# The first forty microseconds of an mLSTM kernel: gates loaded in two parts, differences moved into ScalarE's exponentials, one transposition cut in three

## The chip, the cores and the metric

One core of one Trainium2 chip runs the whole program. The metric is the device time of one execution in microseconds. TensorE (PE) multiplies matrices; PEld is its loading of weights; VectorE (DVE), ScalarE (ACT) and GpSimd (POOL) do the elementwise work; SyncE (SP) issues the DMAs.

## What is computed

Three stages follow one another; the change touches the start of the first. Per head (32 of them, 768 steps, dimension 40):

```python
for t in range(S):
    m_new = np.maximum(f_gate[:, :, t] + m, i_gate[:, :, t])
    f_stab = np.exp(f_gate[:, :, t] + m - m_new)
    i_stab = np.exp(i_gate[:, :, t] - m_new)
    m = m_new
    C = f_stab * C + i_stab * outer(v_t, k_t)
    n = f_stab * n + i_stab * k_t
    y[:, :, t] = sigmoid(o_gate) * (C @ q_t) / max(abs(n @ q_t), 1)
```

Then comes a soft mixture of experts over the 3072 tokens (softmax over tokens and over slots, 8 experts), then a two-layer network with a squared ReLU.

## The kernel before

The mLSTM is done in chunks of 128 steps: six chunks (NC = 6) for each of eleven groups of three heads. A unit is one group and one chunk. For a unit, TensorE spreads a row of gate sums over the partitions (`e_mb`, tile ps_mb), ScalarE makes weights of them with exponentials (`e_exp`, tile w), GpSimd clears the upper triangle (`e_sel`), TensorE multiplies keys with queries (`e_st`, tile ps_st), VectorE multiplies the two (`e_pm`, tile p), TensorE applies the result to the values (`e_av`, `e_inter`, tile ps_o) and updates the state (`e_u`, tile ps_st).

The gate rows (32 heads, three copies on 96 partitions) are prepared ahead for two chunks at a time by `prep(c0, c1)`: chunks 0 and 1 as "1", 2 and 3 as "2", 4 and 5 as "3". The order of all this is written out by hand in the string `START`, whose tokens are run one by one in program order; each engine then executes its own instructions strictly in that order. The part before the first `|` runs ahead of the loop over units; the parts behind it run one in each of the first turns of the loop. A token is:

- `~n`: n warming matmuls of TensorE, whose results nobody reads; they write the bank `ltb` (ps_lt).
- `1f`: scan of the forget gates (VectorE). `1i`: input gate less that sum. `1m`: copy of a carry and scan of the maximum. `1p`: the maximum carried in (mprev). `1h`: the negated maximum in bf16 (ScalarE). `1r`, `1u`, `1l`, `1v`: what bf16 left over, split into two more bf16 rows (VectorE, ScalarE, VectorE, ScalarE).
- `1a`, `1b`: two differences (G means GpSimd instead of VectorE), and `1A`, `1B`: their exponentials (ScalarE). `1q`: transposition of the three gate rows by TensorE into `ltb` and a copy out of it to `qt3`.
- `D0`: the four steps of the decay of a chunk pair, one at each call (VectorE and ScalarE; VectorE; TensorE; VectorE).
- `T`, `M`, `E`, `K`, `P` with a number: `e_st`, `e_mb`, `e_exp`, `e_sel`, `e_pm` of that unit. `W`: `e_wv`, the values times a gate column of `qt3` (GpSimd). `X`: a copy.

The loop begins with `e_u` of unit 0, then `e_mb` of unit 3 and `e_st` of unit 2, and so on. There are two ps_st banks; `e_u` of unit 0 takes the bank that `e_pm` of unit 0 (P0) has just read. The keys are loaded in three blocks of a group (one DMA for each head j) and in two halves of the sequence; the blocks off the diagonal of `kbd` (in par0 and par1, par_70 and par_71 in the instruction rows) are cleared to zero first. DMAs use eight semaphores in turn (DMAHW0 to DMAHW7): SyncE issues the ninth when the first has landed, and so on.

Of the kernel before, what the change touches and what calls it, by code (L numbers as in the profile page):

```python
# [13 lines left out]
AF = mybir.ActivationFunctionType  # L14
# [3 lines left out]
NEG = -1e30  # L18
# [14 lines left out]
W8 = 1  # L33
WO = (3, 6, 9)
LAST = {3: "PADNgGG", 2: "gGGA", 1: ""}
START = "~36 1f 1i 1m 1h 1p 1b 1aG 1B 1r 1u 1A 1v D0 2f 1l T0 T1 1q M0 2i E0 W0 K0 D0 M1 E1 ~6 2m D0 2p 2b 2aG K1 W2 P0 2h D0 2B 2r 2u P1 M2 2v E2 2A 2l K2 ~7 | 3f 3i D1 ~6 | D1 2q 3m 3h 3p | D1 3b 3aG 3B 3r | 3u D1 3A 3l 3v | D2 3q | D2 | D2 | D2 X |"
REBIAS = 2.0**-112


# [5 lines left out]
def kernel(  # L45
# [231 lines left out]
    nc.sync.dma_start(out=fg.rearrange("p c s -> p (c s)"), in_=f_gate)  # L277
    nc.sync.dma_start(out=ig.rearrange("p c s -> p (c s)"), in_=i_gate)
    halves = slice(0, S // 2), slice(S // 2, S)
    nc.vector.memset(kbd[0][:, :, halves[0]], 0.0)  # L280
    for g, cs in ((1, halves[0]), (0, halves[1]), (1, halves[1])):
        z = kbd[g][:, :, cs]
        nc.scalar.activation(z, ident[0 : 3 * D, 0:1].unsqueeze(2).to_broadcast(list(z.shape)), AF.Copy, scale=0.0)
    for g in range(2):
        load_kb(g, halves[0])
        load_q(g, halves[0])
        load_kv(g)
    for g in range(2):
        load_kb(g, halves[1])
        load_q(g, halves[1])  # L290
    nc.sync.dma_start(out=phs, in_=phi)
    load_x(0, range(NC))
# [101 lines left out]

    def prep_dec(c0, c1):
# [1270 lines left out]
```

## Time and profile before

| | us |
|---|---|
| median of three runs (378.13 to 380.14) | 379.23 |
| the profiled execution | 378.38 |
| its span on the core | 376.6 |

The profiled execution took 378.38 us, of which its span is 376.6 us and 1.8 us lie around it. It is 0.85 us below the median. Times in the rows are counted from the start of the span.

### The profile page before, as it was taken

Reading aid. Unit: us, or ns where it says so; the run is one execution under the profiler, and the core shown is the slowest. Engines: PE = TensorE matmul, PEld = TensorE weight load, DVE = VectorE, ACT = ScalarE, POOL = GpSimd, SP = SyncE. Lnnn points to the kernel's source line nnn. Section 1 sums busy time; section 2 is a strip of 40 time slices with the busy share of each in tenths; the row PEclk is TensorE's granted clock in tenths of the full one; section 3 lists DMA queues with packets and bytes.
Section 4 is the critical chain, followed back from the end, with each engine's and each line's share of the span. In section 5 each row is a group of like instructions: output and inputs, shape, how many; then the busy total and the mean of one; then the engine's idle time right before and its main releaser. Section 6 shows DMA issues by size and latency. Waiting matters only on the chain.

```text
span 376.6 us, 10714 instructions
## 1 busy us (share of the span) xinstructions
PE 364.9 (97%) x4203; PEld 324.9 (86%) x4203; DVE 264.7 (70%) x597; ACT 259.0 (69%) x594; POOL 99.8 (26%) x205
## 2 busy tenths in 40 slices
PE   7999998999999999999999999999999999999996
PEld 6789887888879885345899999999999999999995
DVE  7979888979998487786799655555555555555551
ACT  7798775669666865775798766576576666667661
POOL 5666976766677474000000000000000000000000
PEclk9999999999999999999999999999999999999999
DMA  6797997899969999994000100020020002002002
GB/s 175 248 333 231 286 328 212 275 317 372 319 190 400 339 365 297 342 376 177 3 0 2 62 9 1 2 70 0 2 70 2 1 2 70 3 0 71 0 3 70
DMA packets 19547, 56.72 MB, mean 151 GB/s; under 512 B 2481, under 2 KB 7561, under 8 KB 19113
## 3 DMA queue, kind: packets, MB, share of 16 engines
q1 hardware_dynamic: 19497, 56.04, 43.6%
q8 instruction: 33, 0.54, 0.6%
q14 instruction: 17, 0.14, 0.1%
HBM read 52.10 MB, written 3.93 MB: 149 GB/s over the span
## 4 chain that ended last, share of the span: by engine, by line
PE 81%; DVE 9%; POOL 3%; issue 3%; ACT 1%; DMA 1%; SPq 0%; DVEq 0%; POOLq 0%
PE ps_mb L1561 19%; PE ps_st L1561 17%; PE ps_lt L1561 9%; PE ps_st L474 8%; PE ps_o L1488 4%; PE ps_o L559 3%; PE ps_o L574 3%; PE ps_st L1376 2%; PE ps_st L502 2%; DVE p L486 2%; PE ps_m L1488 2%; PE ps_mb L443 2%; DVE x L656 1%; PE ps_lt L725 1%; PE ps_st L1224 1%
## 5 line engine op out<-in xcount | busy, mean ns | idle before, releaser
L1512 DVE CAST hi<-ring 128x512 fp32r<-128x512 f32 x93 | 39.7, 427 | 62.0 <-ACT ring L1511 51.8
L1513 DVE TENSOR_TENSOR los<-ring,hi 128x512 fp32r<-128x512 f32 x96 | 66.4, 692 | 9.8
L457 ACT ACTIVATE w<-ps_mb,qt 128x128 f32<-128x128 f32 x192 | 56.3, 366 | 15.1 <-PE ps_mb L443 7.5
L1493 ACT ACTIVATE ring<-ps_o 128x512 f32<-128x512 f32 x64 | 38.3, 598 | 35.0 <-PE ps_o L1488 35.0
L1511 ACT ACTIVATE ring<-ring 128x512 f32<-128x512 f32 x93 | 58.8, 632 | 3.0
L474 PE MATMUL ps_st<-par 120*128 120x128 f32 (+1 forms) x384 | 56.9, 284 | 0.7 <-DMA par<-in_q_t_dram 0.6
L1561 PE MATMUL ps_mb<-wohlh,hi 128*128 128x320 f32 x160 | 49.5, 310 | 0.0
L1561 PE MATMUL ps_mb<-wohll,hi 128*128 128x320 f32 x160 | 49.3, 309 | 0.0
L1561 PE MATMUL ps_mb<-wohlh,los 128*128 128x320 f32 x160 | 49.2, 309 | 0.0
L474 PEld LDWEIGHTS ps_st<-par 120*128 120x128 f32 (+1 forms) x384 | 47.9, 192 | 1.1 <-DVE ring L370 0.9
L1561 PE MATMUL ps_st<-wohll,hi 128*128 128x320 f32 x144 | 44.7, 310 | 0.0
L1561 PE MATMUL ps_st<-wohlh,hi 128*128 128x320 f32 x144 | 44.6, 309 | 0.0
L1561 PE MATMUL ps_st<-wohlh,los 128*128 128x320 f32 x144 | 44.5, 309 | 0.0
L464 POOL TENSOR_SCALAR_AFFINE_SELECT w<-w 128x384 f32<-128x384 f32 (+1 forms) x66 | 36.4, 551 | 17.1 <-ACT w L457 11.2
L486 DVE TENSOR_TENSOR p<-ps_st,w 128x384 f32<-128x384 f32 (+1 forms) x66 | 35.5, 537 | 4.2 <-POOL w L464 3.3
L1493 ACT ACTIVATE ring<-ps_m 128x512 f32<-128x512 f32 x32 | 19.2, 600 | 19.0 <-PE ps_m L1488 19.0
L1561 PEld LDWEIGHTS ps_mb<-wohll,hi 128*128 128x128 f32 x160 | 29.9, 187 | 1.5
L1561 PEld LDWEIGHTS ps_mb<-wohlh,los 128*128 128x128 f32 x160 | 30.0, 188 | 0.0
L1561 PEld LDWEIGHTS ps_mb<-wohlh,hi 128*128 128x128 f32 x160 | 30.0, 188 | 0.0
L1561 PEld LDWEIGHTS ps_st<-wohll,hi 128*128 128x128 f32 x144 | 27.0, 187 | 2.1 <-issue 0.6
L1561 PEld LDWEIGHTS ps_st<-wohlh,los 128*128 128x128 f32 x144 | 27.1, 188 | 0.0
L1561 PEld LDWEIGHTS ps_st<-wohlh,hi 128*128 128x128 f32 x144 | 27.1, 188 | 0.0
(318 smaller groups left out, 760.7 us busy)
## 6 DMA issues: line engine op xcount, KB each, us to landing
ring<-in_w_dram SPq DMA_DIRECT2D x22, 640.0 KB
stage<-in_w_in_dram SPq DMA_DIRECT2D x10, 512.0 KB
par<-in_w_dram SPq DMA_DIRECT2D x6, 640.0 KB
out_dram<-ring SPq DMA_DIRECT2D x24, 160.0 KB
par<-in_v_s_dram SPq DMA_DIRECT2D x9, 369.0 KB
par<-in_k_s_dram SPq DMA_DIRECT2D x9, 360.0 KB
x<-in_o_gate_dram SPq DMA_DIRECT2D x9, 320.0 KB
par<-in_k_t_dram SPq DMA_DIRECT2D x23, 120.0 KB
```

Of the source, the lines that this page charges most:

```text
L457: nc.scalar.activation(w[:, j, :], mb[:, 128 * j : 128 * j + 128], AF.Exp, bias=qt3[:, c, h0 + j : h0 + j + 1])
L464: nc.gpsimd.affine_select(out=w, in_=w, pattern=[[0, nh], [1, 128]], compare_op=ALU.is_ge, fill=0.0, base=0, channel_multiplier=-1)
L474: nc.tensor.matmul(st[:, 128 * j : 128 * j + 128], lhsT=kbd[g % 2][0:nd, j, ts_], rhs=qin[g][0:nd, ts_], start=True, stop=True,)
L486: nc.vector.tensor_tensor(out=p, in0=sts.pop((g, c))[:, 0 : nh * 128].rearrange("p (n t) -> p n t", n=nh), in1=ws.pop((g, c)), op=ALU.mult,)
L559: nc.tensor.matmul(pos[g, c // 2][:, o0 : o0 + nv], lhsT=qin[g][0:nd, 128 * c : 128 * c + 128], rhs=cbds[g, c - 1][0:nd], start=True, stop ...
L574: nc.tensor.matmul(po[t0 : t0 + 32, o0 : o0 + DV], lhsT=p[:, j, t0 : t0 + 32], rhs=vin[g][:, c, j, :], start=True, stop=True,)
L1488: nc.tensor.matmul(t, lhsT=gst[n][:, 128 * k : 128 * k + 128], rhs=cst[tg], start=True, stop=True)
L1493: nc.scalar.activation(r, t, AF.Relu)
L1511: nc.scalar.activation(r, r, AF.Square)
L1512: nc.vector.tensor_copy(hi, r)
L1513: eng.tensor_tensor(out=lo, in0=r, in1=hi.bitcast(F32), op=ALU.subtract)
L1561: nc.tensor.matmul(acc[u][:, 0:DM], lhsT=l_[:, 128 * u : 128 * u + 128], rhs=wohl[r_, f // 8][:, f % 8, :], start=(f == 0 and a == 0), sto ...
```

## The change

The gates are loaded for chunks 0 and 1 first and for the other four later, v and k of the first two groups likewise; the rest of the loads stand in `load_second`, token `L`. The clearings by ScalarE become six of one head each, and the last clearing goes to GpSimd. The two differences `a` and `b` are gone: the exponentials take them as bias, with one instruction for each chunk, and a small negation `1n` takes their place. The transposition of the first chunk pair becomes three (`1s` for the first 32 rows through bank m, `1t` for the second, `1w` for the third through `ltb`), of which the second and third are copied out by VectorE. Two reductions and a copy of VectorE (`heads`, token `H`) move from the front into the sequence. `START` is written anew.

```diff
-START = "~36 1f 1i 1m 1h 1p 1b 1aG 1B 1r 1u 1A 1v D0 2f 1l T0 T1 1q M0 2i E0 W0 K0 D0 M1 E1 ~6 2m D0 2p 2b 2aG K1 W2 P0 2h D0 2B 2r 2u P1 M2 2v E2 2l 2A K2 ~7 | 3f 3i D1 ~6 | D1 2q 3m 3h 3p | D1 3b 3aG 3B 3r | 3u D1 3A 3l 3v | D2 3q | D2 | D2 | D2 X |"
+START = "~13 1f 1i 1s ~9 1m 1h 1p 1n 1r 1u 1v H D0 1l T0 T1 ~1 1B 2f M0 1t E0 2i W0 K0 D0 M1 E1 ~5 2m 2h 2p 2n P0 H D0 2r D0 1A 2u K1 W2 P1 M2 2v E2 2l 2A K2 1w L ~7 | 3f 3i D1 2B ~6 | D1 2q 3m 3h 3p 3n | D1 3A 3r | 3u D1 3B 3l 3v | D2 3q | D2 | D2 | D2 X |"
...
+    def load_gates(c0, c1):
+        for t, src in ((fg, f_gate), (ig, i_gate)):
+            nc.sync.dma_start(
+                out=t[:, c0:c1].rearrange("p c s -> p (c s)"), in_=src[:, L * c0 : L * c1]
+            )
+
+    def zero(g, j, cs):
+        z = kbd[g][:, j, cs]
+        nc.scalar.activation(z, ident[0 : 3 * D, 0:1].to_broadcast(list(z.shape)), AF.Copy, scale=0.0)
+
+    load_gates(0, 2)
...
+    for g in (1, 0):
+        for j in range(3):
+            zero(g, j, halves[1 - g])
+    load_kb(0, halves[0])
+    load_q(0, halves[0])
+    load_kv(0, 0, 2)
+    load_gates(2, NC)
+    load_kb(1, halves[0])
+    load_q(1, halves[0])
+    load_kv(1, 0, 2)
...
-        nc.vector.tensor_copy(selF[rs, :], ident[rs, rs])
-    nc.vector.tensor_copy(sel96, selF[0:96])
+        if r < 3:
+            nc.vector.tensor_copy(sel96[rs, :], ident[rs, rs])
+        nc.gpsimd.tensor_copy(selF[rs, :], ident[rs, rs])
+    nc.gpsimd.memset(kbd[1][:, :, halves[1]], 0.0)
...
-        def qt():
+        def qt(r=0, n=96):
             t = ltb
             for c in range(c0, c1):
-                nc.tensor.transpose(t[:, 96 * (c - c0) : 96 * (c - c0) + 96], q3[:, c, :], ident[0:96, 0:96])
-            nc.scalar.copy(qt3[:, cs, :], t[:, 0 : 96 * w].rearrange("p (c s) -> p c s", s=96))
+                nc.tensor.transpose(t[:, n * (c - c0) : n * (c - c0) + n], q3[0:n, c, :], ident[0:n, 0:n])
+            tv = t[:, 0 : n * w].rearrange("p (c s) -> p c s", s=n)
+            (nc.vector.tensor_copy if r else nc.scalar.copy)(qt3[:, cs, r:n], tv[:, :, r:])
...
         def exp(r):
-            return lambda: nc.scalar.activation(q3[r : r + 32, cs], q3[r : r + 32, cs], AF.Exp)
+            def go():
+                for c in range(c0, c1):
+                    src, b, k = (q3, mlast, 1.0) if r == 32 else (mm, mprev, -1.0)
+                    nc.scalar.activation(
+                        q3[r : r + 32, c], src[r : r + 32, c], AF.Exp, bias=b[r : r + 32, c], scale=k
+                    )
+
+            return go
```

Three places in the engines' instruction streams. The first is TensorE's, from the third decay step of the first chunk pair (L410, L455 after) to `e_u` of unit 0 (L502, L547 after); lines left out are `e_mb` and further warming matmuls. Before:

```order
L410 MATMUL ps_m<-ring 120x22 [waits DVE_49]
...
L443 MATMUL ps_mb<-M_112,sel_105 128x128
L200 LDWEIGHTS ident
L200 MATMUL ps_lt<-ident 128x256
...
L502 MATMUL ps_st<-wv,par_70 120x123 [waits DMAHW7_49,DVE_49]
```

In the changed kernel the same stretch has the transpositions of `1w` (L374) in it:

```order
L455 MATMUL ps_m<-ring 120x22 [waits DVE_49,PE_49]
...
L374 MATMUL ps_lt<-ident,ring 128x96 [waits Activation_49] x2
L200 LDWEIGHTS ident
L200 MATMUL ps_lt<-ident 128x256 [waits DVE_49]
...
L547 MATMUL ps_st<-wv,par_70 120x123 [waits DMAHW7_49,PE_49,Pool_49]
```

What moved: a transposition now stands ahead of the seven warming matmuls of `~7`, it uses their bank, and the first of them now waits for VectorE.

The second place is VectorE's, from P0 (L531, `p<-ps_st,w`) on. In the changed kernel:

```order
L531 TENSOR_TENSOR p<-ps_st,w 128x384 [waits Pool_49]
L350 COPY ring<-ring 32x120
L419 SCALAR_TENSOR_TENSOR ring<-ring,M_112 96x256 [waits Activation_49]
L463 COPY dec_114<-ps_m 120x11x2 [waits PE_49]
L531 TENSOR_TENSOR p<-ps_st,w 128x384 [waits Pool_49]
L401 TENSOR_TENSOR M_112<-ring,M_112 32x256 [waits Activation_49]
L376 COPY qt_113<-ps_lt 128x2x32 [waits PE_49]
L563 TENSOR_TENSOR ring<-ps_st,hm 120x123 [waits PE_49]
```

Before, the same place reads (L486 is P0 and P1, L376 is `2r`, L370 is `2l`):

```order
L486 TENSOR_TENSOR p<-ps_st,w 128x384 [waits PE_49,Pool_49]
L418 COPY dec_114<-ps_m 120x11x2 [waits PE_49]
L376 SCALAR_TENSOR_TENSOR ring<-ring,M_112 96x256 [waits Activation_49]
L486 TENSOR_TENSOR p<-ps_st,w 128x384 [waits Pool_49]
L370 TENSOR_TENSOR M_112<-ring,M_112 32x256 [waits Activation_49]
L518 TENSOR_TENSOR ring<-ps_st,hm 120x123 [waits PE_49]
```

What moved: the copy of `heads` (L350) came in behind P0, and the copy out of `1w` (L376) behind `2l`.

The third place is GpSimd's, around W0 (L475, `wv<-par_70,qt`) in the changed kernel; L343 are the copies taken over from VectorE, L344 is the clearing of the second half of par_71, L509 is K0 and K1.

```order
L338 COPY selJ<-ident 32x4x8 [waits Pool_49]
L343 COPY selF<-ident 32x32 x4
L344 MEMSET par_71 120x3x384 [waits DMAHW3_49,DMAHW4_49,Activation_49,Pool_49]
L475 TENSOR_TENSOR wv<-par_70,qt_113 128x246 [waits DMAHW6_49,DVE_49]
L509 AFFINE_SELECT w<-w 128x384 [waits Activation_49] x2
```

Before, between the copy to selJ and W0 stood the difference `1a`; now a clearing stands there that waits for two DMAs, the key blocks of heads j = 1 and 2 of group 1 (the eleventh and twelfth loads, DMAHW3 and DMAHW4).

## Rows read from the trace of the kernel before

**Rows 1.** The page, the chain that ended last: shares by engine.
```profile
PE 81%; DVE 9%; POOL 3%; issue 3%; ACT 1%; DMA 1%; SPq 0%; DVEq 0%; POOLq 0%
```

**Rows 2.** The chain from 0 to 60 us: start us, us, what.
```profile
1.25 3.77 DMA ring<-in_i_gate_dram
...
5.11 0.42 DVE ring L370
...
11.63 0.57 DVE p L486
...
12.24 0.47 PE ps_st L502 x2
...
13.02 0.91 PE ps_st L474 x6
13.93 0.66 PE ps_lt L200 x6
...
22.03 0.40 DVE p L486
...
22.68 0.48 PE ps_o L559 x2
```

**Rows 3.** VectorE's groups, 0 to 14 us: busy us, mean ns of one, idle before.
```profile
L376 DVE SCALAR_TENSOR_TENSOR ring<-ring,M 96x256 f32<-96x256 f32 x2 | 1.5, 738 | 0.0
L360 DVE TENSOR_TENSOR_SCAN ring<-ring 96x256 f32<-96x256 f32 x2 | 1.4, 717 | 0.1
...
L370 DVE TENSOR_TENSOR ring<-ring 32x256 f32<-32x256 f32 x2 | 1.2, 602 | 0.1
L486 DVE TENSOR_TENSOR p<-ps_st,w 128x384 f32<-128x384 f32 x2 | 1.1, 550 | 0.0
...
L370 DVE TENSOR_TENSOR ring<-ring 96x256 f32<-96x256 f32 x2 | 0.8, 421 | 0.3 <-DMA ring<-in_i_gate_dram 0.2
L370 DVE TENSOR_TENSOR M<-ring,M 32x256 bf16<-32x256 f32 x2 | 0.8, 416 | 0.1
...
L321 DVE COPY ring<-ring 32x120 f32<-32x120 f32 x1 | 0.3, 266 | 0.0
...
L418 DVE COPY dec<-ps_m 120x22 f32<-120x22 f32 x1 | 0.2, 171 | 0.0
```

**Rows 4.** GpSimd's groups, 0 to 14 us.
```profile
L430 POOL TENSOR_TENSOR wv<-par,qt 128x246 f32<-128x246 f32 x2 | 1.4, 717 | 3.7 <-ACT qt L351 2.4 <-DMA par<-in_v_s_dram 1.3
L464 POOL TENSOR_SCALAR_AFFINE_SELECT w<-w 128x384 f32<-128x384 f32 x2 | 1.1, 531 | 0.1
L303 POOL MEMSET ring<- 96x768 f32 x1 | 0.7, 738 | 0.0
```

**Rows 5.** Timeline, 0 to 22 us: SyncE's issues and TensorE's first e_st.
```profile
2.15 2.92 SPq L210 DMA_DIRECT2D par<-in_k_t_dram  x3
...
5.12 0.36 SPq L215 DMA_DIRECT2D par<-in_q_t_dram  x1
...
5.52 0.43 SPq L225 DMA_DIRECT2D par<-in_v_s_dram  x1
...
7.70 1.57 PE L474 MATMUL ps_st<-par 120*128 120x128 f32 x12 [0.61 <-DMA par<-in_q_t_dram]
```

**Rows 6.** Timeline, 0 to 22 us: a copy out of ps_lt, what follows, W0 and `2p`.
```profile
9.48 0.32 ACT L351 COPY qt<-ps_lt 128x192 f32<-128x192 f32 x1 [0.17 <-PE ps_lt L350]
...
9.85 0.82 PE L200 MATMUL ps_lt<-ident 128*128 128x256 bf16 x6
...
9.93 0.83 POOL L430 TENSOR_TENSOR wv<-par,qt 128x246 f32<-128x246 f32 x1 [2.37 <-ACT qt L351]
...
10.41 0.38 DVE L365 TENSOR_TENSOR ring<-ring 96x2 f32<-96x2 f32 x1
```

**Rows 7.** The warming matmuls' durations (min/median/max ns), in 2 to 3 us.
```profile
L200 PE MATMUL ps_lt<-ident x7: 417/418/418, 1.6 to 2.9; 128*128 128x256 bf16 x7
```

**Rows 8.** The same, in 5 to 6 us.
```profile
L200 PE MATMUL ps_lt<-ident x12: 272/273/273, 4.7 to 5.9; 128*128 128x256 bf16 x12
```

More of the change, by code (lines that the diff above doesn't have):

```diff
@@ L35 @@
 LAST = {3: "PADNgGG", 2: "gGGA", 1: ""}
-START = "~36 1f 1i 1m 1h 1p 1b 1aG 1B 1r 1u 1A 1v D0 2f 1l T0 T1 1q M0 2i E0 W0 K0 D0 M1 E1 ~6 2m D0 2p 2b 2aG K1 W2 P0 2h D0 2B 2r 2u P1 M2 2v E2 2A 2l K2 ~7 | 3f 3i D1 ~6 | D1 2q 3m 3h 3p | D1 3b 3aG 3B 3r | 3u D1 3A 3l 3v | D2 3q | D2 | D2 | D2 X |"
+START = "~13 1f 1i 1s ~9 1m 1h 1p 1n 1r 1u 1v H D0 1l T0 T1 ~1 1B 2f M0 1t E0 2i W0 K0 D0 M1 E1 ~5 2m 2h 2p 2n P0 H D0 2r D0 1A 2u K1 W2 P1 M2 2v E2 2l 2A K2 1w L ~7 | 3f 3i D1 2B ~6 | D1 2q 3m 3h 3p 3n | D1 3A 3r | 3u D1 3B 3l 3v | D2 3q | D2 | D2 | D2 X |"
 REBIAS = 2.0**-112
@@ L276, with load_second @@
     nc.scalar.activation(dm, dm, AF.Exp)
-    nc.sync.dma_start(out=fg.rearrange("p c s -> p (c s)"), in_=f_gate)
-    nc.sync.dma_start(out=ig.rearrange("p c s -> p (c s)"), in_=i_gate)
+    def load_gates(c0, c1):
[7 more added lines that the diff above has]
+    load_gates(0, 2)
     halves = slice(0, S // 2), slice(S // 2, S)
     nc.vector.memset(kbd[0][:, :, halves[0]], 0.0)
[L281 to L292, printed above, removed]
+    for g in (1, 0):
[8 more added lines that the diff above has]
+    load_kv(1, 0, 2)
+    def load_second():
+        for g in range(2):
+            load_kv(g, 2, NC)
+            load_kb(g, halves[1])
+            load_q(g, halves[1])
+        nc.sync.dma_start(out=phs, in_=phi)
+        load_x(0, range(NC))
     nc.gpsimd.memset(gj, 1.0)
@@ L299 @@
     rst = gt(96, [NC, L])
-    nc.gpsimd.memset(rst, 1.0)
-    nc.gpsimd.memset(rst[:, :, 0:1], 0.0)
     dl = gt(96, [NC, L])
-    nc.gpsimd.memset(dl, 0.0)
-    nc.gpsimd.memset(dl[:, 0, 0:1], NEG)
     mprev = gt(96, [NC, 1])
-    nc.gpsimd.memset(mprev, NEG)
+    mlast = gt(96, [NC, 1])
+    for c0, c1 in ((0, 2), (2, NC)):
+        nc.gpsimd.memset(rst[:, c0:c1], 1.0)
+        nc.gpsimd.memset(rst[:, c0:c1, 0:1], 0.0)
+        nc.gpsimd.memset(dl[:, c0:c1], 0.0)
+        if c0 == 0:
+            nc.gpsimd.memset(dl[:, 0, 0:1], NEG)
+            nc.gpsimd.memset(mprev, NEG)
     nc.gpsimd.memset(hm, 1.0)
@@ L318, with heads @@
     nc.gpsimd.tensor_copy(selJ[:, :, 0:8], ident[0:32, 0:32].rearrange("p (j i) -> p j i", j=4))
-    nc.vector.tensor_reduce(out=gmask, in_=gj, axis=AX.X, op=ALU.add)
-    nc.vector.tensor_reduce(out=gs3, in_=gj.rearrange("p g j -> p j g"), axis=AX.X, op=ALU.add)
-    nc.vector.tensor_copy(hsel, gs3.unsqueeze(2).to_broadcast([32, 3, D]))
     for r in range(4):
         rs = slice(32 * r, 32 * r + 32)
-        nc.vector.tensor_copy(selF[rs, :], ident[rs, rs])
-    nc.vector.tensor_copy(sel96, selF[0:96])
+        if r < 3:
+            nc.vector.tensor_copy(sel96[rs, :], ident[rs, rs])
+        nc.gpsimd.tensor_copy(selF[rs, :], ident[rs, rs])
+    nc.gpsimd.memset(kbd[1][:, :, halves[1]], 0.0)
+    def heads():
+        nc.vector.tensor_reduce(out=gmask, in_=gj, axis=AX.X, op=ALU.add)
+        nc.vector.tensor_reduce(out=gs3, in_=gj.rearrange("p g j -> p j g"), axis=AX.X, op=ALU.add)
+        yield
+        nc.vector.tensor_copy(hsel, gs3.unsqueeze(2).to_broadcast([32, 3, D]))
     def flat(t):
@@ L343, in prep, with qt32 @@
         tail = mm[:, c0 - 1, L - 1 : L] if c0 else 0.0
-        last = mm[32:64, cs, L - 1 : L].to_broadcast([32, w, L])
         tt = {"D": nc.vector.tensor_tensor, "G": nc.gpsimd.tensor_tensor}
-        def qt():
+        def qt(r=0, n=96):
             t = ltb
             for c in range(c0, c1):
-                nc.tensor.transpose(t[:, 96 * (c - c0) : 96 * (c - c0) + 96], q3[:, c, :], ident[0:96, 0:96])
-            nc.scalar.copy(qt3[:, cs, :], t[:, 0 : 96 * w].rearrange("p (c s) -> p c s", s=96))
+                nc.tensor.transpose(t[:, n * (c - c0) : n * (c - c0) + n], q3[0:n, c, :], ident[0:n, 0:n])
+            tv = t[:, 0 : n * w].rearrange("p (c s) -> p c s", s=n)
+            (nc.vector.tensor_copy if r else nc.scalar.copy)(qt3[:, cs, r:n], tv[:, :, r:])
+        def qt32():
+            t = bank("m")
+            for c in range(c0, c1):
+                nc.tensor.transpose(t[:, 32 * (c - c0) : 32 * (c - c0) + 32], q3[0:32, c, :], ident[0:32, 0:32])
+            nc.scalar.copy(qt3[:, cs, 0:32], t[:, 0 : 32 * w].rearrange("p (c s) -> p c s", s=32))
         def f_scan():
@@ L370, in sub, with last @@
             return lambda e="D": tt[e](out=o_, in0=a, in1=b, op=ALU.subtract)
+        def last():
+            nc.vector.tensor_scalar(
+                out=mlast[32:64, cs], in0=mm[32:64, cs, L - 1 : L], scalar1=-1.0, scalar2=None, op0=ALU.mult
+            )
         def exp(r):
-            return lambda: nc.scalar.activation(q3[r : r + 32, cs], q3[r : r + 32, cs], AF.Exp)
+            def go():
+                for c in range(c0, c1):
+                    src, b, k = (q3, mlast, 1.0) if r == 32 else (mm, mprev, -1.0)
+                    nc.scalar.activation(
+                        q3[r : r + 32, c], src[r : r + 32, c], AF.Exp, bias=b[r : r + 32, c], scale=k
+                    )
+            return go
         def rest():
@@ L383, in prep @@
             "p": prev,
-            "a": sub(q3[64:96, cs], mprev[64:96, cs].to_broadcast([32, w, L]), mm[64:96, cs]),
-            "b": sub(q3[32:64, cs], q3[32:64, cs], last),
+            "n": last,
             "A": exp(64),
@@ L392, in prep @@
             "q": qt,
+            "s": qt32,
+            "t": lambda: qt(32, 64),
+            "w": lambda: qt(64),
         }
@@ L914 @@
     begin["W"] = lambda n: e_wv(units[int(n)][0], 0, 2)
+    hd = heads()
+    begin["H"] = lambda: next(hd, None)
+    begin["L"] = load_second
     begin["X"] = lambda: nc.vector.tensor_copy(sel4, selF.unsqueeze(1).to_broadcast([128, 4, 32]))
```

## The prediction

> **What bounds the kernel now.** I read the page's chain that ended last first, then its pieces in time order for the first 60 us, then the engines' groups and the timeline of the first 22 us. The chain is 81% TensorE [rows 1]. It begins with a load: the input gates are issued at 1.25 us and land 3.77 us later, at 5.02, and `1i` starts at 5.11. From there VectorE carries it until P0 (start 11.63, length 0.57), and P0 releases `e_u` of unit 0 at 12.24. From 13.02 on TensorE's pieces follow one another; the first that is not TensorE's stands at 22.03 (VectorE's p and a sum behind it, TensorE goes on at 22.68) [rows 2]. So the opening is a latency, and what it costs is read at one point: **the start of TensorE's stream, 12.24 us**. What starts that stream later moves everything behind it, since between 13.02 and 22.03 there is no pause in which it could catch up.
>
> **The gate loads.** The first two gate loads carry a third of the bytes. How long a 96 KB load takes to land no row shows. The nearest is the first query load, 192 KB, issued at 5.12 and waited for until 7.70: 2.58 us [rows 5]. That is the upper end, so `1i` starts by about 1.25 + 2.58 = 3.83 instead of 5.11. The lower end is VectorE: its clearing of par0 releases the first key load at 2.15 [rows 5], then come three small copies (0.17 each, as the smallest copy measured) and the `1f` scan (0.72) [rows 3], so 3.4. I take 3.75, a gain of 1.35 us.
>
> **From `1i` to P0 on VectorE.** In program order, by the durations of rows 3: `1i` 0.42, carry 0.17, scan 0.72, `1p` 0.17, `1n` 0.17 (an operation of the size of the other small ones), `1r` 0.74, two reductions 0.17 each, decay 0.17, `1l` 0.42, `2f` 0.72, copy of `1t` 0.17, `2i` 0.42, decay 0.17, carry 0.17, scan 0.72, `2p` and `2n` 0.17 each: 6.0 us. The two subtractions `b` (0.60 on the mean) are gone from it. Two waits come in: `1l` stands behind ScalarE's `1u`, and the copy of `1t` behind two transpositions that wait for the exponentials; I give them 0.4 together (both ends: nothing, and 0.9). So VectorE is at P0 at 3.75 + 6.4 = 10.15. Before, the same stretch was 11.63 - 5.11 = 6.52: nearly all of the gain here is that of the loads.
>
> **From the loads to P0 on GpSimd.** GpSimd's new clearing of par1 waits for two key loads, the eleventh and twelfth on SyncE's queue, and W0, K0 and K1 stand behind it. The third key block is issued after ten others at about 0.40 each (5.12 to 5.52 in [rows 5]), from 2.15 on, at 6.15. For 60 KB I take 2.2 us to landing (ends: 1.5, being a third of the query load's bytes, and the 3.77 of the gates in a busy queue [rows 2]): 8.35. The clearing has 1152 elements a partition; at 0.738 for 768 [rows 4] it is 1.1, so it ends at 9.45. W0 0.72 and K0 0.53 [rows 4] make 10.75 with hand-overs, after VectorE is ready. **P0 starts at 10.8**, 0.8 us sooner than before. The clearing's cover would be the time in which W0 waits for `1t`; that runs out at about 8.4 (4.2 of the work above and the waits), and without the clearing VectorE's 10.15 would set P0: 0.65 us of the gain is spent here.
>
> **Behind P0.** Before, this was the end: `e_u` followed P0 at once. Now `1w` puts a transposition into the bank of the warming matmuls, its copy stands on VectorE behind `2l`, and the seven warming matmuls in front of `e_u` wait for that copy. That such a wait is real the trace shows at the old transposition: the copy out of ps_lt ends at 9.48 + 0.32 = 9.80 and the six warming matmuls in that bank start at 9.85 [rows 6]. Queued on VectorE from P0 to the copy: P0 0.55, the copy of `heads` 0.27, `2r` 0.74, decay 0.17, P1 0.55, `2l` 0.42, the copy 0.17 [rows 3], 2.87, with seven hand-overs of 0.03 about 3.05. That is 13.85. P1 needs K1, which follows K0 by 0.53 and is ready by 11.4; `2l` needs ScalarE's `2u`, done under P1. Six warming matmuls take 0.66 before the next work starts [rows 2], so seven take 0.77, with 0.05 to start. **`e_u` of unit 0 starts at 14.65, not at 12.24: 2.4 us later.** Queued behind it is all of TensorE's work. The matmuls left out of the front (36 become 13, 9 and 1) cost and give nothing: they ended ahead of the wait for the query load [rows 5].
>
> The remaining edits are hidden as long as TensorE's stream sets the end: one exponential for each chunk instead of one for two on ScalarE, the difference `a` gone from GpSimd, the second parts of gates, v and k. The latter are used by `e_wv` and the second preparation microseconds after their issue; if they were late, `2f` would stand behind them and all of the second preparation with it.
>
> **Both ends.** Without any wait for ScalarE or GpSimd, VectorE's own work from 3.4 on is 6.0 + 3.05, and `e_u` starts at 13.3: 1.0 us later than before. With a landing of 3.77 us for the key block, P0 starts at 12.4 and `e_u` at 16.2: 4.0 later.
>
> One more price lies between. `2p`, a sum of two columns, took 0.38 us while W0 ran on GpSimd from 9.93 to 10.76, and ended 0.03 after it [rows 6]; other small operations take 0.17 [rows 3]. If each of `2m`, `2p` and `2r` waits so for a GpSimd instruction, 0.2 to 0.6 are added. I leave them inside the range. The Trainium skill (SBUF — State Buffer, Who interferes with whom) says that a VectorE instruction with two SBUF inputs contends with a GpSimd instruction that reads SBUF, one being blocked for the whole of the other; by that rule the sum would be some 0.4 us more, as an estimate, and the row of `2p` agrees with it.
>
> **The rivals.**
> *Not slower.* TensorE's late start is made up behind it: the pauses of TensorE after 22 us (0.6 at 22.03 to 22.68 [rows 2], and those in the 19% of the chain that are not TensorE's [rows 1]) belong to the other engines' own load, and these come there sooner, since their preparations have lost `a` and `b`. It decides from 2.4 us of such pauses on; then the time is that of before, 379.2, or up to 0.9 less, if P0's 0.8 counts as well. Against it: at 22.03 the p follows the e_st that TensorE has just ended, so a later TensorE makes it later. Chance 0.15.
> *The clock falls.* In the changed kernel TensorE waits about 2.2 us for the decay matmul (its hsel copy now stands behind P0) and again over 1 us for the copy of `1w`. At the start of the run the warming matmuls take 418 ns [rows 7] and later 272 [rows 8], the lower and the higher clock level, after some 3.3 us of matmuls without a pause (from 1.42). If the pauses bring the lower level back, a stretch like that is paid again at half speed behind `e_u`: 1.6 us more, 382.8. For it: the rows show no pause so long, so they don't exclude it; against it: after the pause of 0.61 that ends at 7.70 [rows 5] the next warming matmuls keep their pace, six in 0.82 [rows 6]. Chance 0.13. The Trainium skill (TensorE: Matmul & The Clock Gate, What's actually happening) says the half clock is the default state and activity releases it, so it speaks for this rival; no row here shows a fall.
> *The loads gain nothing*, because the latency is the same for 96 KB as for 288: `1i` stays at 5.02, P0 starts at 11.6 and `e_u` at 15.45, 3.2 later; 382.0. The query row speaks against it. Chance 0.05.
>
> **How the numbers follow.** The sum is made against the profiled execution: 378.38 + 2.4 = 380.8. That run lies 0.85 under the median of those shown, against which it would be 379.23 + 2.4 = 381.6; I forecast 381.2, between them. Chance of this case 0.67; its own range is 379.8 (1.0 later) to 382.8 (4.0 later). The range with the others is 379.2 to 383.2. About 0.5%, 1.9 us, is what a measurement of this kernel can tell from no change. Of the forecast's 0.67, 0.25 lies below that bound (the low end of the sum). With the clock and the idle loads, slower is 0.42 + 0.18 = 0.60; the not-slower rival gives mostly no change: same 0.34, faster 0.06.
>
> **What would show it.** Right: `1i` starts near 3.75; GpSimd's clearing starts with the landing of a key load after 8 us; the first of seven warming matmuls starts right behind VectorE's copy into qt, after P1 and `2l`; `e_u` starts between 13.3 and 16.2, and the stream behind it has the spacing of before. Wrong: `e_u` starts at 12.2 or sooner, or starts late but the stretch at 22 us and those behind it lie where they lay.

## The result: 1.3% slower, and the profile after

The changed kernel took 384.34 us (383.97 to 385.25, six runs) against 379.43 us (378.13 to 380.21) of the kernel before: a ratio of 1.0134, 95% interval 1.0111 to 1.0156, so 4.9 us more. 381.2 was forecast, and 383.2 was the end of the range. The profiled execution took 384.18 us with a span of 382.4 us, 5.8 more than before.

The page of the changed kernel, the chain that ended last by engine, beside [rows 1]:

```profile
PE 81%; DVE 5%; POOL 5%; DMA 3%; issue 2%; ACT 1%; SPq 1%; POOLq 0%; DVEq 0%
```

GpSimd and the DMAs have taken shares from VectorE. Where, the chain from 0 to 60 us says (start, us, what), beside [rows 2]:

```profile
5.05 4.08 DMA ring<-in_i_gate_dram
9.23 0.42 DVE ring L401
...
11.42 0.60 POOL wv L475
12.02 0.50 POOL w L509
12.54 0.56 DVE p L531
...
14.93 0.24 DVE qt L376
15.21 1.65 PE ps_lt L200 x7
16.86 0.41 PE ps_st L547 x2
```

The load in the chain is now the second piece of the input gates, issued at 5.05 and landed 4.08 us later; then come W0 and K0 on GpSimd, P0, the copy of `1w`, the seven warming matmuls, and `e_u` of unit 0. The timeline of the first 22 us, beside [rows 5, 6] (in brackets: idle before, and what ended it):

```profile
3.92 0.42 DVE L401 TENSOR_TENSOR ring<-ring 96x256 f32<-96x256 f32 x1
...
5.60 1.05 SPq L210 DMA_DIRECT2D par<-in_k_t_dram  x3
...
8.24 0.69 DVE L385 TENSOR_TENSOR_SCAN ring<-ring 96x256 f32<-96x256 f32 x1 [1.15 <-DMA ring<-in_f_gate_dram]
...
10.28 1.06 POOL L344 MEMSET par<- 120x1152 f32 x1 [3.78 <-ACT w L502]
...
12.54 0.56 DVE L531 TENSOR_TENSOR p<-ps_st,w 128x384 f32<-128x384 f32 x1 [1.19 <-POOL w L509]
...
13.42 0.35 PE L455 MATMUL ps_m<-ring 32*120 32x22 f32 x2 [3.59 <-DVE ring L350]
...
15.21 1.65 PE L200 MATMUL ps_lt<-ident 128*128 128x256 bf16 x7 [0.69 <-DVE qt L376]
...
16.66 0.62 PE L547 MATMUL ps_st<-wv,par 128*120 128x123 f32 x2
```

The reader is to see five things. `1i` starts at 3.92 instead of 5.11. `2f` then waits 1.15 us for the second piece of the forget gates. The clearing of par1 starts at 10.28 only (ScalarE's instruction named there ended at 10.24, just before; the first experiment's row names the load). TensorE stands idle for 3.59 us before the decay matmul. And the seven warming matmuls start right behind VectorE's copy, and take 1.65 us. `e_u` starts at 16.66, 4.42 later than before.

The next view is of windows (from:to, sum, busy TensorE with its number of matmuls, granted clock, DMA share, GB/s):

```profile
13.00:14.00 1.00, 0.58 (x6) 0.85 0.97 296
14.00:15.00 1.00, 0.53 (x4) 0.50 1.00 363
15.00:20.00 5.00, 4.79 (x24) 0.50 1.00 352
20.00:21.00 1.00, 1.00 (x10) 0.74 1.05 414
```

Behind the idle stretch the granted clock falls to half, the 1.2 GHz level, at about 13.7 us, and rises again at about 20.5. The warming matmuls before `e_u` therefore have the duration of [rows 7] and not that of [rows 8] (min, median, max ns):

```profile
L200 PE MATMUL ps_lt<-ident x7: 372/421/421, 15.2 to 16.4; 128*128 128x256 bf16 x7
```

Further on the stream has the spacing of before, only later. I read it at one place throughout: the sixth `e_u`, the first behind the pause at 22 us. It starts at 23.00 before and at 28.32 after, 5.32 later, and the later ones keep 5.32 to 5.34 up to 96 us. The last 0.5 us of the 5.8 by which the span grew lies behind that, and executions of one and the same kernel differ by more (378.13 to 380.21 before).

### The profile page after: what moved, and what is told of

The parts are those of the page before. It is cut to its first block, busy times and chain, and to the rows that moved or that the text cites. A ratio compares the mean times of both kernels' runs of the same rounds, so it can differ in the third digit from the quotient of the medians.

```text
span 382.4 us, 10722 instructions
## 1 busy us (share of the span) xinstructions
PE 367.7 (96%) x4193; PEld 326.3 (85%) x4193; DVE 263.5 (69%) x597; ACT 260.3 (68%) x603; POOL 99.3 (26%) x210
## 4 chain that ended last, share of the span: by engine, by line
PE 81%; DVE 5%; POOL 5%; DMA 3%; issue 2%; ACT 1%; SPq 1%; POOLq 0%; DVEq 0%
PE ps_mb L1609 18%; PE ps_st L1609 17%; PE ps_lt L1609 9%; PE ps_st L519 8%; PE ps_o L1536 4%; PE ps_o L604 3%; PE ps_o L619 3%; PE ps_st L547 2%; PE ps_st L1424 2%; PE ps_m L1536 2%; PE ps_mb L488 2%; DMA par<-in_v_s_dram 2%; POOL w L509 2%; POOL numr L693 1%; PE ps_lt L770 1%
## 5 line engine op out<-in xcount | busy, mean ns | idle before, releaser
L502 ACT ACTIVATE w<-ps_mb,qt 128x128 f32<-128x128 f32 x192 | 56.6, 370 | 16.1 <-PE ps_mb L488 7.3
L519 PE MATMUL ps_st<-par 120*128 120x128 f32 (+1 forms) x384 | 57.9, 287 | 0.2 <-issue 0.2
L519 PEld LDWEIGHTS ps_st<-par 120*128 120x128 f32 (+1 forms) x384 | 48.8, 194 | 0.4 <-issue 0.4
L509 POOL TENSOR_SCALAR_AFFINE_SELECT w<-w 128x384 f32<-128x384 f32 (+1 forms) x66 | 36.2, 549 | 23.9 <-ACT w L502 13.0
L531 DVE TENSOR_TENSOR p<-ps_st,w 128x384 f32<-128x384 f32 (+1 forms) x66 | 35.5, 538 | 6.6 <-POOL w L509 5.9
```

What stands on the lines that cost most here:

```text
L502: nc.scalar.activation(w[:, j, :], mb[:, 128 * j : 128 * j + 128], AF.Exp, bias=qt3[:, c, h0 + j : h0 + j + 1])
L509: nc.gpsimd.affine_select(out=w, in_=w, pattern=[[0, nh], [1, 128]], compare_op=ALU.is_ge, fill=0.0, base=0, channel_multiplier=-1)
L519: nc.tensor.matmul(st[:, 128 * j : 128 * j + 128], lhsT=kbd[g % 2][0:nd, j, ts_], rhs=qin[g][0:nd, ts_], start=True, stop=True,)
L531: nc.vector.tensor_tensor(out=p, in0=sts.pop((g, c))[:, 0 : nh * 128].rearrange("p (n t) -> p n t", n=nh), in1=ws.pop((g, c)), op=ALU.mult,)
```

## The experiments

All times stand against runs of the kernel before on the same chip. "First" and "sixth" are the starts of `e_u` of unit 0 and of the sixth `e_u` in the profiled execution; "clock" says whether the granted clock fell to half there after the opening. One execution is one reading: a load of the opening lands up to 0.8 us sooner or later in another (last section).

| kernel | median us | ratio, 95% interval | first | sixth | clock |
|---|---|---|---|---|---|
| before | 379.43 | 1 | 12.24 | 23.00 | high |
| after | 384.34 | 1.0134 (1.0111 to 1.0156) | 16.66 | 28.32 | fell |
| e1_no_hold | 382.25 | 1.0081 (1.0052 to 1.0109) | 14.41 | 26.17 | fell |
| e2_clear_apart | 383.38 | 1.0111 (1.0077 to 1.0145) | 16.23 | 27.52 | fell |
| e3_keep_warm | 382.05 | 1.0075 (1.0053 to 1.0098) | 15.88 | 25.99 | high |
| e4_gates_whole | 384.34 | 1.0137 (1.0099 to 1.0174) | 17.70 | 28.69 | fell |
| v1_repaired | 379.88 | 1.0019 (1.0002 to 1.0036) | 12.47 | 22.85 | high |
| v2_repaired_t1 | 380.39 | 1.0038 (1.0017 to 1.0059) | 13.08 | 23.45 | high |
| e5_bias_alone | 379.37 | 1.0002 (0.9986 to 1.0018) | 12.02 | 22.44 | high |
| e6_split_alone | 381.51 | 1.0053 (1.0034 to 1.0073) | 15.46 | 25.87 | fell (in two runs of six) |
| e7_repaired_no_warm | 380.68 | 1.0035 (1.0019 to 1.0051) | 12.84 | 25.90 | fell |
| v3_gates_first | 379.47 | 0.9998 (0.9981 to 1.0015) | 12.61 | 22.85 | high |
| v4_w2_late | 379.65 | 1.0020 (0.9999 to 1.0042) | 12.33 | 22.98 | high |

My theory was that the loss is the start of TensorE's stream and has three parts: the hold by `1w`'s copy, the late clearing, and the fallen clock. e1 and e2 each take one of them away, e3 keeps the clock up, e4 undoes the split of the gates, and v1 takes away the three together.

**e1_no_hold**: the changed kernel without the seven warming matmuls that wait for `1w`'s copy.

```diff
-... 2l 2A K2 1w L ~7 | 3f 3i ...
+... 2l 2A K2 1w L | 3f 3i ...
```

> The changed kernel without the seven warming matmuls between 1w and the first e_u, so that nothing in front of e_u waits for VectorE's copy out of ps_lt. Theory (the hold, the clearing's wait and the fallen clock each cost): e_u of unit 0 follows the transpositions of 1w at about 14.6 us instead of 16.66, but the half clock (13.7 to 20.5 us) stays, so only about half of the 2.1 us is won, 383.2 us against 384.3. Rival (the clock alone makes the kernel late, the hold lies beside it): e_u starts sooner and the time stays at 384.3.

The sixth `e_u` comes 2.15 sooner than after, and the time with it (382.25). The seven matmuls had waited 0.69 us for the copy and then taken 1.45 us up to `e_u`, 2.14 together; so what e1 takes away is the wait and the matmuls themselves. That I expected only half of it back was wrong. The timeline of this run also names what the clearing waits for:

```profile
10.17 1.06 POOL L344 MEMSET par<- 120x1152 f32 x1 [3.67 <-DMA par<-in_k_t_dram]
```

**e2_clear_apart**: the last clearing as three instructions of one head each, none of which spans a block that a load writes.

```diff
-    nc.gpsimd.memset(kbd[1][:, :, halves[1]], 0.0)
+    for j in range(3):
+        nc.gpsimd.memset(kbd[1][:, j, halves[1]], 0.0)
```

> The changed kernel with GpSimd's last clearing cut into three of one head each, which no longer waits for key loads. Theory: W0 starts right after the copy of 1t (9.1 us instead of 11.42), P0 is then set by VectorE at about 11.1 instead of 12.54, and the warming matmuls start about 1.4 us sooner. TensorE's pause ahead of the decay matmul shrinks from 3.6 to about 2.1 us: if the clock then stays high the whole gain is 3.1 us (381.2 us), if it falls all the same 1.4 us (382.9). Rival (the late second gate loads set P0, not the clearing): P0 stays at 12.5 and the time at 384.3.

The timeline, lines of the clearings, the scan behind `2i`, and P0:

```profile
6.57 1.14 POOL L345 MEMSET par<- 120x384 f32 x3
...
10.06 0.91 DVE L392 TENSOR_TENSOR_SCAN ring<-ring 96x256 f32<-96x256 f32 x1
...
11.91 0.56 DVE L532 TENSOR_TENSOR p<-ps_st,w 128x384 f32<-128x384 f32 x1
```

The clearings wait for nothing, but P0 comes at 11.91 and not at 11.1, 0.63 sooner than after. With W0 and K0 earlier they run beside VectorE's scan, which takes 0.91 instead of 0.75, and VectorE sets P0. The late clearing costs 0.8 us in this execution (sixth `e_u` 27.52); the medians alone do not show it, since the two intervals overlap.

**e3_keep_warm**: 35 warming matmuls instead of 5 over TensorE's idle stretch.

```diff
-... M1 E1 ~5 2m 2h ...
+... M1 E1 ~35 2m 2h ...
```

> The changed kernel with 35 instead of 5 warming matmuls ahead of the decay matmul, which fill TensorE's pause of 3.6 us and end at about 12.9, before the wait for VectorE does. Theory: the granted clock stays at its upper level, the seven warming matmuls take 0.77 us instead of 1.45, the stretch behind e_u its old length, and the time falls by 1.7 us to 382.6; the start of the seven stays at 15.2. Rival (the slow stretch is not the clock, or the clock does not hang on this pause): no change, 384.3, or slower if the added matmuls run past 13.4.

The decay matmul and the seven warming matmuls on its timeline:

```profile
13.33 0.35 PE L455 MATMUL ps_m<-ring 32*120 32x22 f32 x2 [0.17 <-DVE ring L350]
...
15.12 0.93 PE L200 MATMUL ps_lt<-ident 128*128 128x256 bf16 x7 [0.99 <-DVE qt L376]
```

P0 and the copy stand where they stood in the changed kernel, the matmuls take 0.93 instead of 1.65, and the clock stays high through. The sixth `e_u` comes 2.33 sooner: that is the price of the clock.

**e4_gates_whole**: the gates in one load each again, the rest as changed.

```diff
-    load_gates(0, 2)
+    load_gates(0, NC)
...
-    load_gates(2, NC)
```

> The changed kernel with the gates loaded whole at the start, as before, v and k still in two parts. Theory (the split of the gates moves a wait from 1i to 2f and sends the key loads later): 1i starts at 5.1 instead of 3.92, 2f no longer waits 1.15 us for its load, the key loads are issued 0.9 us sooner and so the clearing starts near 9.4 instead of 10.28; P0 at about 11.7, 0.8 us sooner, 383.5 us. Rival (the split is worth its 1.2 us at 1i): P0 later than 12.54 and a time of 384.9 or more.

The clearing and the copy of `1t` on its timeline:

```profile
8.55 1.06 POOL L343 MEMSET par<- 120x1152 f32 x1 [1.29 <-DMA par<-in_k_t_dram]
...
10.57 0.22 DVE L375 COPY qt<-ps_lt 128x64 f32<-128x64 f32 x1 [1.73 <-PE ps_lt L373]
```

At P0 the rival was right, it comes 1.0 later: `2f` and the clearing wait less, but `1i` starts at 5.00, and the copy of `1t` waits 1.73 for TensorE. In the time neither was: 384.34, as with the split, and the profiled execution (385.35) is the slowest of the four. So in this order of work the split is neither a gain nor a loss that the medians could tell.

**v1_repaired**: all three parts undone, the loads in pieces and the exponentials with a bias kept.

```diff
-... 1u 1v H D0 1l ... E1 ~5 2m 2h 2p 2n P0 H D0 2r ... 2A K2 1w L ~7 | 3f 3i D1 2B ~6 | D1 2q ...
+... 1u 1v H H D0 1l ... E1 ~5 D0 2m 2h 2p 2n P0 2r ... 2A K2 L ~18 | 3f 3i D1 2B ~6 1w | D1 2q ...
...
-    nc.gpsimd.memset(kbd[1][:, :, halves[1]], 0.0)
+    for j in range(3):
+        nc.gpsimd.memset(kbd[1][:, j, halves[1]], 0.0)
```

> The changed kernel with its waits taken away: both steps of `heads` stand before the first decay matmul's place, so the decay matmul comes with the key block's exponentials and not behind P0; `1w` stands after the first unit's e_u, so the warming matmuls wait for no copy and run (18 of them) up to P0; the last clearing is three instructions of one head each. All of the loads in pieces and the exponentials with a bias stay. My theory (what the change lost is the start of TensorE's stream, and its three parts are the late clearing, the copy and decay matmul behind P0, and the low granted clock after TensorE's pause): P0 starts at about 11.9, as with the clearings apart, or a little sooner; e_u of unit 0 at about 12.5, 0.25 after the kernel before; clock at the high level throughout; time 379.2, the same as before within 0.5%. Rival (something else of the change costs too, in the 370 us behind the opening, such as the smaller packets or ScalarE's shorter instructions): e_u at 12.5 and still 380.5 or more, with the shift growing after 23 us.

`2f`, P0 and the first `e_u` on its timeline:

```profile
8.00 0.69 DVE L386 TENSOR_TENSOR_SCAN ring<-ring 96x256 f32<-96x256 f32 x1 [0.83 <-DMA ring<-in_f_gate_dram]
...
11.81 0.56 DVE L532 TENSOR_TENSOR p<-ps_st,w 128x384 f32<-128x384 f32 x1
...
12.47 0.44 PE L548 MATMUL ps_st<-wv,par 128*120 128x123 f32 x2
```

As the theory said: P0 at 11.81, `e_u` at 12.47, the clock high, and the time the kernel before's within 0.5%. The sixth `e_u` comes 5.47 sooner than after; the three parts singly make 2.15 + 0.80 + 2.33 = 5.28. That the two agree so closely is in part luck. e1 and e3 both take away the time that the seven matmuls lose to the half clock (0.72, 1.65 against 0.93), so the sum has it twice; and v1 also moves the copy of `heads` and the decay matmul ahead of P0, which no run did alone. The rival's further cost does not show: at the tenth `e_u` v1 and the kernel before both stand at 32.30, so no shift grows there.

**v2_repaired_t1**: v1 with the second key block's `e_st` behind the transpositions of `1t`.

```diff
-... 1l T0 T1 ~1 1B 2f M0 1t E0 2i ...
+... 1l T0 ~1 1B 2f M0 1t T1 E0 2i ...
```

> As v1_repaired, but T1 (the second key block's transposition) stands behind `1t` on TensorE, so that the transpositions of `1t` wait for no key load of the second half. Theory: the copy of `1t` is some 0.5 us sooner, VectorE's chain with it, P0 at about 11.3 to 11.5, e_u at about 12.0, and the time about 0.4 us under v1_repaired: 378.8. Rival (P0 waits for GpSimd's W0 and K0 and not for VectorE's chain): P0 as in v1_repaired, no difference.

`2f` on its timeline:

```profile
8.82 0.69 DVE L386 TENSOR_TENSOR_SCAN ring<-ring 96x256 f32<-96x256 f32 x1 [1.65 <-DMA ring<-in_f_gate_dram]
```

A miss: the forget gates landed 0.8 later than in v1, at the same issue (4.59), so the transpositions had nothing to win, and P0 came at 12.42. The time is not told apart from v1's.

**e5_bias_alone** and **e6_split_alone**: the kernel before with one part of the change each.

```diff
-... 1h 1p 1b 1aG 1B 1r ... 2p 2b 2aG K1 W2 P0 ...
+... 1h 1p 1n 1B 1r ... 2p 2n K1 W2 P0 ...
```

```diff
+    load_gates(0, 2)
...
-        load_kv(g)
+        load_kv(g, 0, 2)
+        if g == 0:
+            load_gates(2, NC)
```

> The kernel before with one part of the change: the differences of `a` and `b` as bias of ScalarE's exponentials, one chunk at a time. Theory: VectorE loses `2b` (0.6) between the scan and P0, and P0 is then held by K0 and K1 of GpSimd, so P0 at about 11.35 instead of 11.63 and the time 0.25 to 0.3 under the kernel before: 378.7, the same within 0.5%. Rival (ScalarE's twice as many exponentials, each with its fixed part, come late for the transposition of the second chunk): e_u at 12.3 or later, 379.2 or more.

> The kernel before with one part of the change: gates, v and k loaded in two pieces each, the order of the start as before. Theory: `1i` starts at about 3.9 instead of 5.11, but `2f` stands ahead of `1l` on VectorE and waits for the second piece of the forget gates, which lands at about 8.2, and `2i` for that of the input gates at about 9.1; P0 comes at about 12.0, 0.4 later than before, and the time is about 379.4: the same within 0.5%. Rival (the second pieces land before they are asked for): `1i` 1.2 sooner carries through to P0 and e_u, 377.9.

P0 on the timeline of e5_bias_alone:

```profile
11.41 0.56 DVE L497 TENSOR_TENSOR p<-ps_st,w 128x384 f32<-128x384 f32 x1 [0.66 <-POOL w L475]
```

And `2f` on that of e6_split_alone:

```profile
10.44 0.76 DVE L362 TENSOR_TENSOR_SCAN ring<-ring 96x256 f32<-96x256 f32 x1 [2.98 <-DMA ring<-in_f_gate_dram]
```

e5 is as expected: P0 waits for K0, `e_u` is 0.22 sooner, and the time is the same. In e6 the direction is right and the size wrong: P0 comes at 13.95, 2.3 later than before instead of 0.4, and the time is 2.0 longer where none was expected. SyncE issues the second forget gates at 6.49 only, behind the held-up key loads, and they land 3.95 later. In the profiled execution the clock falls too, for 3.4 us, but not in most: the mean granted clock is 0.996 in two of the six runs and 0.999 or 1.000 in the other four, which still took 380.3 to 381.6 us, against 379.1 in the middle for the kernel before. So the late load makes e6 slow without the clock, too.

**e7_repaired_no_warm**: v1 without its 18 warming matmuls, so that TensorE pauses again.

```diff
-... 2A K2 L ~18 | 3f 3i ...
+... 2A K2 L | 3f 3i ...
```

> v1_repaired without the 18 warming matmuls that stand between the second key block's M1 and the first unit's e_u. Nothing on the other engines moves, so P0 and e_u of unit 0 should start as there, at 11.8 and 12.5; TensorE then stands idle from about 10.6 to 12.5, 1.9 us, instead of the 3.6 us of the changed kernel. Theory (the fall of the granted clock after TensorE's pause is what cost the changed kernel some 2.3 us): the clock falls to the low level within some us and stays for several, each e_u from 14 to 23 us comes 1 to 2 us later than in v1_repaired, and the time is 381.0 to 381.5. Rival (a pause of this length is forgiven): the clock stays at the high level and the time is that of v1_repaired, 379.9.

> e7_repaired_no_warm once more, for a second profiled execution: in the first the clock fell and the sixth e_u stood 3.05 us behind that of v1_repaired, but the medians differ by 0.8 only. If the clock falls in some executions and not in others (TensorE's pause ends with P0, and that hangs on a load that lands at a different time in each execution): the clock may stay high here, the sixth e_u at about 23, and the time under 380. If it falls each time: the sixth e_u at about 25.9 again, and then the medians' small difference is not explained by it.

Windows of the first profiled execution, columns as above:

```profile
11.00:12.00 1.00, 0.00 (x0) 1.00 0.82 272
12.00:13.00 1.00, 0.16 (x1) 0.55 1.00 289
13.00:18.00 5.00, 5.00 (x27) 0.50 0.89 270
```

The clock fell with a pause of 1.85 us, and in the second profiled execution (381.57 us) with one of 1.50. In both the sixth `e_u` came 3.05 behind v1's, 0.4 to 0.5 of it ahead of the first `e_u` (12.84 and 12.98 against 12.47). The medians, though, are 0.8 us apart (380.68, under the 381.0 expected), with intervals that overlap, where the profiled executions are 2.3 to 2.7 apart.

The mean granted clock of each run says most of why. All twelve runs of e7 have 0.991 to 0.995, v1's have 0.998 to 1.000. Six of e7's have 0.991, the value of both profiled executions; their median is 381.2 us. The other six have 0.994 or 0.995, near the 0.996 of e6's profiled execution, whose clock was low for 3.4 us instead of 6.8; their median is 380.3. v1's median is 379.9, and its profiled execution (378.83) was one of its fastest. So by these means the clock fell in every run of e7, in half of them for less time, and it cost about 1.3 us and 0.4 us in the whole time. A mean does not show where in the span the clock was low, and why 3.05 at the sixth `e_u` is only 1.3 at the end stays open.

**v3_gates_first** and **v4_w2_late**: v2 with the second forget gates issued ahead of the queries; then W2 of GpSimd moved behind K2 as well.

```diff
+    load_gate(2, NC, fg, f_gate)
     load_q(0, halves[0])
+    load_gate(2, NC, ig, i_gate)
     load_kv(0, 0, 2)
-    load_gates(2, NC)
```

```diff
-... 2u K1 W2 P1 M2 2v E2 2l 2A K2 L ...
+... 2u K1 P1 M2 2v E2 2l 2A K2 W2 L ...
```

> v2_repaired_t1 with the second piece of the forget gates issued ahead of the first queries and that of the input gates right behind them, ahead of v and k. Theory (in both repaired kernels P0 waits for VectorE's chain, and that waits 0.8 to 1.7 us in `2f` for the second forget gates): `2f` starts at about 7.2 to 7.4 without a wait, the queries land about 0.5 later and T0 starts at 7.1, the copy of `1t` comes at 8.6, P0 at 11.2 and e_u of unit 0 at 11.9, 0.3 sooner than in the kernel before: 378.9, at the edge of what can be told. Rival (the queries, a piece later, hold up T0 and with it the transpositions of `1t`, W0 and the key blocks): the copy of `1t` at 9.5 or later and P0 at 12 or later, 379.9 or more.

> v3_gates_first with GpSimd's product W2 (of the third unit, used at about 17.6) moved from its place behind K1 to behind K2. Theory (VectorE's operations between the scan and P0 take longer there because GpSimd works on the same tiles' memory at the same time: `2n` 0.57 beside W2 where it takes 0.14 to 0.17 with GpSimd at rest): `2n` takes 0.15 to 0.2, P0 starts at about 11.4 instead of 11.81, with the scan at 0.92 beside W0 and K0 as before. The first e_u may still stand behind the 18 warming matmuls, which end at 12.77 there; the time falls by 0.4 at most, to 379.1 to 379.5, and cannot be told from either. Rival (`2n` is long for another reason, its own operands): it keeps 0.57 and P0 its 11.8.

`2f`, the scan, `2n` (L409) and P0 on the timeline of v3_gates_first:

```profile
7.21 0.69 DVE L390 TENSOR_TENSOR_SCAN ring<-ring 96x256 f32<-96x256 f32 x1
...
9.84 0.92 DVE L396 TENSOR_TENSOR_SCAN ring<-ring 96x256 f32<-96x256 f32 x1
...
11.21 0.57 DVE L409 TENSOR_SCALAR ring<-ring 32x2 f32<-32x2 f32 x1
11.81 0.56 DVE L536 TENSOR_TENSOR p<-ps_st,w 128x384 f32<-128x384 f32 x1
```

`2n` and P0 on that of v4_w2_late:

```profile
10.93 0.16 DVE L409 TENSOR_SCALAR ring<-ring 32x2 f32<-32x2 f32 x1
11.12 0.56 DVE L536 TENSOR_TENSOR p<-ps_st,w 128x384 f32<-128x384 f32 x1
```

In v3 `2f` waits for nothing, as expected, and the copy of `1t` starts at 8.68 (8.6 was expected), but P0 stays at v1's 11.81. From that copy to P0 VectorE needs 3.1 us, as it needed 3.0 in v1, because the operations there stand beside GpSimd's. With W2 away `2n` takes 0.16 instead of 0.57, and P0 comes at 11.12, 0.5 sooner than before; of the 0.69 against v3, 0.41 is `2n`, and 0.28 is that the copy of `1t` started sooner (8.40), behind queries that landed sooner. Nothing of it arrives: `e_u` stands behind the 18 warming matmuls (12.33), and the sixth `e_u` at 22.98 is where it was. Neither time can be told from the kernel before, so no version here beats it.

## Why the prediction was wrong in size

The direction and the place held: TensorE's stream starts late and stays late. The sum had 2.4 us for that, and the runs show 4.42 at the first `e_u` and 5.32 at the sixth. Of the 2.9 that it lacked, 1.7 lie ahead of P0 (the landing of the key block and VectorE's own way, both taken too short), 0.3 between P0 and `e_u`, and 0.9 behind `e_u`, where the sum put the half clock at nothing and left it to a rival. Point by point:

- **The gate loads.** Right: 3.92 where 3.75 was taken, 5.11 before.
- **From `1i` to P0 on VectorE: too short.** 6.4 us were taken, and VectorE was ready for P0 at 11.35 (12.54 less the wait of 1.19), 7.4 after `1i`. The difference is `2f`'s wait of 1.15, which the prediction named and then priced at nothing ("used ... microseconds after their issue"). In v1 and v2 this wait, 0.83 and 1.65, takes much of the gain of the loads. Beside W0 and K0 VectorE then slows down as well: from the start of `1t`'s copy to P0 it takes 3.0 us in v1 and e2, where it was ready after 2.5 in the changed kernel. In v3, without the wait of `2f`, the copy of `1t` waits 0.78 for TensorE, whose `e_st` waited for the queries issued later.
- **From the loads to P0 on GpSimd: this step failed.** "For 60 KB I take 2.2 us to landing": the clearing began at 10.28 instead of 8.35. The clearing needs the last two of the three loads in the row at 5.60 (counted from the first gate load they are the twelfth and thirteenth, not the eleventh and twelfth). The last was issued at about 6.3, near the 6.15 taken, and landed some 3.9 us later. I had the bound, 3.77 of [rows 2], and took the query load, which is nearer in bytes, as the nearer row; the lower end of 1.5 follows from no row, since a third of the query load's 2.58 would be 0.9. Other loads were in flight (181 GB/s in 3 to 6 us), which may be why; no run varied that alone. The Trainium skill (DMA: Bandwidth & Descriptors, Anatomy of one DMA — SWDGE (gpsimd) path) fits some 2 us fixed and the bytes on top for a DMA issued from GpSimd, by which 60 KB would take about 2.1 us, as an estimate. These loads are issued by SyncE, and the trace shows far more. Clearing, W0 and K0 took 1.06, 0.60 and 0.50, near what [rows 3, 4] gave:

```profile
L509 POOL TENSOR_SCALAR_AFFINE_SELECT w<-w 128x384 f32<-128x384 f32 x3 | 1.5, 527 | 2.2 <-ACT w L502 2.2
L475 POOL TENSOR_TENSOR wv<-par,qt 128x246 f32<-128x246 f32 x2 | 1.2, 600 | 0.1
L344 POOL MEMSET par<- 120x1152 f32 x1 | 1.1, 1062 | 3.8 <-ACT w L502 3.8
```

These are GpSimd's groups of the changed kernel from 0 to 16 us (busy us, mean ns, idle before). P0 at 12.54 against 10.8 makes 1.7 of the missing 2.0 us at `e_u`. But the clearing is not all of it: with the clearings apart (e2) P0 came at 11.91, set by VectorE. So 0.6 of the 1.7 go to the late landing alone, and 1.1 would have been missing without it.
- **Behind P0.** Right in kind, a little too long: from P0 to the end of the copy 2.6 us (15.16 less 12.54) where 3.05 was taken, because VectorE's operations overlap a little (the copy of `heads` starts at 13.02, P0 ends at 13.10) and `2r` took 0.63 instead of 0.74. Then 1.45 from the first warming matmul to `e_u` where 0.77 was taken: the clock again.
- **The rival "the clock falls"** took place, with 0.13 on it. The sum and the rival were treated as alternatives, though the same step, the copy of `heads` behind P0, brings both. The pause was 3.59 us and not 2.2, but the 2.2 that the prediction itself counted are already longer than the 1.85 and 1.50 with which the clock fell in e7. Its price, 2.33 in e3 (0.78 of it ahead of the first `e_u`), is above the 1.6 that the rival gave. The rival read the lower level from the 418 ns of [rows 7] alone; the granted clock of the kernel before stands at 1.00 there (2 to 3 us), and it is the 421 ns at 0.50 in the changed kernel that bear the reading out. The Trainium skill (TensorE: Matmul & The Clock Gate, What's actually happening) has the half clock as the default state that activity releases; by that rule the trace agrees, at 0.50 from 13.7 to 20.5 us.
- **The rival "not slower"** is excluded: of 5.78 at the fifth `e_u` only 0.46 came back at 22 us.
- **The rival "the loads gain nothing"** is excluded by `1i` at 3.92.
- **"If each of `2m`, `2p` and `2r` waits so for a GpSimd instruction".** The mechanism is shown by v4 at `2n`, which I had not named. In the changed kernel the two instructions of L404 are `1n`, which took 0.16, and `2n`, which took 0.55 and ended with GpSimd's clearing (11.35 and 11.34). In VectorE's groups, 0 to 16 us, only their mean shows:

```profile
L404 DVE TENSOR_SCALAR ring<-ring 32x2 f32<-32x2 f32 x2 | 0.7, 356 | 0.0
```

It cost the changed kernel nothing, since P0 waited 1.19 longer for K0.

## What to carry to other kernels

When work is moved up to where a load has just been moved, price the wait for the load from a row of the same busy stretch, not from the one nearest in bytes, and look for instructions whose operands merely span what a load writes: cut by head, the clearing waited for nothing. When an edit makes TensorE stand idle, put the clock into the sum and not beside it. Read the granted clock of every run, and not only of the profiled one. And fill such a stretch with matmuls that wait for nothing on the path; warming matmuls that share a bank with real work inherit its waits.

## What the hardware showed unexpectedly

- TensorE's granted clock fell with pauses of 3.59 us (the changed kernel), 1.85 and 1.50 us (the two profiled executions of e7). In the first two it then stayed at 0.50 for 6.8 us (from about 13.7 to 20.5, and from 12.1 to 18.9 by the means of the windows at the edges), though TensorE was busy for 5.00 of the 5.00 us from 13 to 18 in e7. With the stretch filled it did not fall (e3, v1). The length of one pause did not decide when it fell. In the second execution of e7 it fell at about 12.0, half a microsecond into the pause of 1.50:

```profile
9.00:11.00 2.00, 0.85 (x7) 1.00 1.03 272
11.00:12.00 1.00, 0.48 (x5) 0.98 0.83 304
12.00:13.00 1.00, 0.02 (x1) 0.50 0.99 258
```

In e4 it was still at 1.00 behind a pause of 2.90 us that ended at 14.46, and fell at about 16.1, near the end of a second pause of 0.99:

```profile
14.00:15.00 1.00, 0.54 (x6) 1.00 0.85 267
15.00:16.00 1.00, 0.26 (x4) 1.00 0.95 344
16.00:18.00 2.00, 1.75 (x9) 0.54 0.97 374
```

- A load that is issued at the same time, in the same order, lands at different times: the second forget gates 3.4 us after their issue in v1, 3.7 in the changed kernel, 4.0 in e7, and 4.2 in v2. The 0.8 us between them is as much as the late clearing cost in e2.
- A VectorE instruction on two columns took 0.57 us beside GpSimd's product and 0.16 without it.
